# Block products of an attention-and-GLU kernel: from three phases of at most two weight sets to a phase of three and a phase of two

## The chip, the cores and the metric

The kernel runs on one NeuronCore of a Trainium2 chip. The metric is the device time of one execution in microseconds; the time before is the median of 3 runs. The engines are named as in the profile: PE (matrix products), DVE, ACT and POOL (elementwise work) and SP (which issues the DMAs).

## The reference

Attention over 4 batches x 8 heads x 768 rows x 64 columns, in which a query sees only the keys of its own hash bucket, and then a gated layer over 3072 tokens:

```python
q_bucket = sum((q @ proj > 0) * powers)            # 6 bits, the same for k
scores = where(q_bucket == k_bucket, q @ k.T / 8, -1e9)
x = softmax(scores) @ v                            # as (3072, 512)
gate = 1 / (1 + exp(-(x @ w_gate)))                # w_gate, w_val: 512 x 1536
return (gate * (x @ w_val)) @ w_out                # w_out: 1536 x 512
```

The weights arrive as 64-bit floats and are converted on the chip. Products are made with three matmuls each (a high part and a low part of both operands, low times low left out).

## The kernel before, in words

`Plan` is a list scheduler that runs while the program is built. Each piece of work is added with a key, an engine (or two, of which one is chosen), an estimated duration, what it comes after, and the tokens that it takes and gives (`stock` says how many there are). `Plan.order()` plays the estimates through and writes every engine's instructions in the order in which it started them. On the chip each engine then runs its own list in that order and waits on semaphores; the estimates have no other effect.

The first half is attention, in 32 units. Beside it the weights are converted: the 1536 columns of the hidden layer are 12 blocks `j` of 128. Blocks 0 and 1 stay in SBUF and are used beside attention (`moe_early`; tiles zg, zv, zo): they give each token's partial sum, written to the DRAM tensor `part`. Blocks 2 to 11 are five sets of two (`SETS`), stored in DRAM (`kept`) in a form for a block product: the tokens of a batch are two halves, the 512 inputs are two halves, and seven products of block sums (`STEPS`, tiles z1 to z7) stand for eight. `converted`, `combined` and `split` make that form. `QUARTERS` says how many sets are converted beside attention; the rest are converted later, beside the block products.

The block products are the second half. `PHASES` says which sets are worked on together; a phase goes over the four batches b, and one (phase, batch) is a pair, built by `moe_pair`:
- `x_pair` loads the four blocks of x (ra) and makes seven operand blocks a11, a12, s1, s2, s3, s4, a22, each in a high and a low part: 4 sums and 7 differences of 128x768, plus 7 casts on ACT;
- `group` runs the seven steps for g (the gate) and for v (the values) of one set: PE writes a z bank (six of them, tag z), ACT copies some out (sn), DVE adds others (L758), and `finish` makes the four results of 128x384: for g a sigmoid, for v the product with the gate (L772), its high part on ACT (gh, L787) and its low part (gl, L789). Where both "pool" and "dve" stand, the planner chooses;
- `part_` makes the output products (yo): 6 token tiles, and for each set 2 blocks x 3 matmuls of 128x512. `ended` fetches the tile's partial sum from DRAM (ob or ol, three buffers each), adds yo on DVE (L893) and stores it, in the last phase to the output.

A set's weights (10 pieces, 4.72 MB) lie in one of two slots and are fetched once per phase by `fetch_piece`. The places that the change and the prediction touch are these functions, the table `PHASES`, `QUARTERS`, and the token list.

Of the kernel before, what the change touches and what calls it, by code (L numbers as in the profile page):

```python
# [169 lines left out]
def lsh_attention_glu_kernel(ctx, tc, q, k, v, proj, w_gate, w_val, w_out, out):  # L170
# [13 lines left out]
    QUARTERS = 3  # L184
# [16 lines left out]
    PHASES = [SETS[i : i + 2] for i in range(0, len(SETS), 2)]  # L201
# [86 lines left out]
    def busy():  # L288
# [5 lines left out]
        ef=4, raw1=1, cv1=1, wk1=2, raw2=1, cv2=1, wk2=1, xr=1, x=1, ob=3, ol=3, sn=4, sg=6, gf=4, sc=1,  # L294
# [27 lines left out]
    def converted(key, n, j, late, which, after, first):  # L322
# [50 lines left out]
        b1 = add(key, "dve", 440, exponent, after=[a], take=[token] if first else [])  # L373
        b2 = add(key, "act", 700, shifted, after=[b1])
        c1 = add(key, "dve", 440, mantissa, after=[b1])
        c2 = add(key, "dve", 700, whole, after=[c1])
        d = add(key, "dve", 700, signed, after=[b2, c2], give=[raw_])
        return z, add(key, "pool", 1300, lambda: scaled(nc.gpsimd), after=[d])

    def split(key, src, to, size, late, after, give, tile_of=None):  # L380
# [17 lines left out]
        low_ = add(key, "pool", 100 + 1200 * part_, low, after=[h], give=give)  # L398
# [22 lines left out]
    def combined(key, n, js, late, after):  # L421
# [27 lines left out]
        x1 = add(key, on(t1), after=[ea, eb])  # L449
        x2 = add(key, on(t2), after=[x1])  # L450
        x3 = add(key, on(t3), after=[eb])
        x4 = add(key, on(t4), after=[x2, x3])
# [20 lines left out]
    def load_x(u, b, g, stored):  # L473
# [21 lines left out]
        for c in range(KC):  # L495
            prev = add(
                FIRST, "act", 415, lambda c=c: high(c), after=[a, prev], take=["x"] if c == 0 else []
            )
            z["ready"].append(add(
                FIRST,  # L500
                [("pool", 960, lambda c=c: low(c, nc.gpsimd)), ("dve", 470, lambda c=c: low(c, nc.vector))],
                after=[prev], give=["xr"] if c == KC - 1 else [],
            ))
# [25 lines left out]
    def gated(u, j, z, done, zsig):  # L529

        def mul():
# [9 lines left out]
            after=[b, g_free[j]],  # L541
# [74 lines left out]
    def x_pair(u, b, last_use):  # L616
# [35 lines left out]
        on = lambda fn: [("pool", 2000, lambda: fn(nc.gpsimd)), ("dve", 960, lambda: fn(nc.vector))]  # L652
# [7 lines left out]
        def summing(name, x, y, op, after):  # L660
            got[name] = add(
                FIRST, on(lambda eng: summed(name, x, y, op, eng)), after=[got[x], got[y]] + after,
                take=["sc"] * (name == "s1"),
            )

        def pieces_of(name):
            h = add(FIRST, "act", 850, lambda: high(name), after=[got[name]], take=[f"x{name}"])
            z["ready"][name] = add(FIRST, on(lambda eng: low(name, eng)), after=[h])
# [25 lines left out]
    pieces = {}  # L694

    def fetch_piece(js, slot, n, m, after, first):

        def go():
            size = HF if m == 3 else DM
            if slot == 1 and n != "o" and m < 3:  # L700
                to = w1.tile([P, 2, size], F32R, name=f"w{n}{m}_{js[0]}", tag=("wg0", "wg1", "wv0", "wv1", "wo0", "wo1")[3 * (n == "v") + m])
            else:
                to = later["x"].tile([P, 2, size], F32R, name=f"w{n}{m}_{js[0]}", tag=f"w{slot}{n}{m}")
# [4 lines left out]
        made[js, n, m] = dma(  # L708
            1e3, CROWDED if first else CROWDED // 4, go, after=[made_piece[key_], later["switch"]] + after, take=[f"w{slot}{n}{m}"]
# [7 lines left out]
    def group(key, u, n, js, slot, x, sig_, final, free_w, hslot, prev):  # L717
# [4 lines left out]

        z, bank, done, told = {}, {}, {}, {}
# [13 lines left out]
        def pe(m):  # L737
            block, piece, half = STEPS[m]
            give = [f"x{block}"] if final else []
            if free_w and m in (2, 6, 3, 4):  # L740
                give = give + [f"w{slot}{n}{piece}"]
            done[m] = add(
                key, "pe", 6 * MM, lambda: step(m), after=[prev, x["ready"][block], made[js, n, piece]], take=["z"], give=give,
# [20 lines left out]
        def finish(where):  # L764
            a = told[where]
            if n == "g":
# [6 lines left out]
            soon = slice(None, None, -1 if final and uu == 0 else 1)  # L773
            b = add(
                FIRST, [("pool", 1040, lambda: mul(nc.gpsimd)), ("dve", 480, lambda: mul(nc.vector))][soon],
                after=[a, sig_[where][1]], give=["sg"],
            )

            def hi():
# [12 lines left out]
                FIRST, [("pool", 1040, lambda: low_(nc.gpsimd)), ("dve", 480, lambda: low_(nc.vector))][soon],  # L792
                after=[c], give=["gf"],
            )

        for m in (1, 2, 5, 6, 3, 7, 4):
# [8 lines left out]
            elif m == 6:  # L805
# [4 lines left out]
                    FIRST, [("pool", 1040, lambda: both(nc.gpsimd)), ("dve", 480, lambda: both(nc.vector))],  # L810
                    after=[told["t"], told["u"]],
# [13 lines left out]
    def moe_pair(key, i, b, prev, before):  # L825
# [4 lines left out]

        sets, last_phase, last_pair = PHASES[i], i == len(PHASES) - 1, b == B - 1
        u = f"{i}_{b}"
        x = x_pair(u, b, None)
        alone = len(sets) == 1
        sigs = []
        for slot, js in enumerate(sets):
            sig_ = {}
            sigs.append(sig_)
            for n in "gv":
                final = slot == len(sets) - 1 and n == "v"  # L840
                prev = group(key, u, n, js, slot, x, sig_, final, last_pair, b % 2 if alone else slot, prev)
        accs = {}

        def part_(t, slot):
            hslot = b % 2 if alone else slot
            if slot == 0:
                accs[t] = ps.tile([P, 512], F32, name=f"yo{t}_{u}", tag="one")
            js = sets[slot]
            uu, tt = t // GT, t % GT
            ts_ = slice(tt * P, (tt + 1) * P)  # L850
            for jj in range(2):
                h_, l_ = hs[hslot, jj, uu]
                oh, ol = pieces[js, "o", jj]
                for q, (a, w) in enumerate(((l_, oh), (h_, ol), (h_, oh))):
                    nc.tensor.matmul(  # L855
                        accs[t], a[:, ts_], w, start=(slot == 0 and jj == 0 and q == 0),
                        stop=(slot == len(sets) - 1 and jj == 1 and q == 2),
                    )

        def out_part(t, slot, prev):  # L860
            uu = t // GT
            ready = [sigs[slot]["h", (jj, uu)] for jj in range(2)] + [made[sets[slot], "o", jj] for jj in range(2)]
            give = []
            if t % GT == GT - 1:
                give += [f"h{b % 2 if alone else slot}{jj}{uu}" for jj in range(2)]
            if last_pair and t == 2 * GT - 1:
                give += [f"w{slot}o{jj}" for jj in range(2)]
            return add(
                key, "pe", 6 * MO, lambda: part_(t, slot), after=[prev] + ready,
                take=["moe", "one"] if slot == 0 else [], give=give,  # L870
            )

        def ended(t, prev):
            z = {}
# [4 lines left out]
            def fetch():  # L879
                pool = mp if where == "ob" else later["t"]  # L880
                z["ob"] = pool.tile([P, DM], F32, name=f"{where}{t}_{u}", tag=where, bufs=stock[where])
                nc.sync.dma_start(z["ob"], part[b][g, tt])

            def store():
# [3 lines left out]
                nc.sync.dma_start(to, z["ob"])  # L888

            a = dma(FIRST, 262144, fetch, after=[parts[b, g, tt], later["switch"]] + in_turn[where], take=[where])  # L890
            in_turn[where] = [a]
            a = add(
                FIRST, "dve", 640, lambda: nc.vector.tensor_add(z["ob"], accs[t], z["ob"]), after=[prev, a],  # L893
                give=["moe", "one"],
            )
            parts[b, g, tt] = dma(FIRST, 262144, store, after=[a], give=[where])

        n_ = len(sets)
# [5 lines left out]
        def outs(prev):  # L904
            for o in order_:
                prev = out_part(*o, prev)
                if o[1] == n_ - 1:
                    ended(o[0], prev)
            return prev

        if not alone:
            return outs(prev), None
        if before:
            prev = before(prev)
        if last_pair:
            return outs(prev), None
# [366 lines left out]
```

## Time and profile before

| | |
|---|---|
| median of 3 runs | 1130.66 us (1125.63 to 1131.22) |
| profiled execution | 1125.4 us, span 1123.3 us |
| granted TensorE clock, mean | 0.971 |
| first block product starts | 574.3 us into the span |
| PE, DVE, ACT, POOL busy, share of the span | 92%, 78%, 51%, 41% |
| DMA moved | 181.23 MB |

The span is what the trace covers; the profiled execution's own time lies 2.1 us above it. A row of the trace for a matmul begins where it is issued and overlaps the next, so two starts give its cost. A wait row has the engine that waits, whom it waited for, the total, how often, and the longest.

### The profile page before, as it was taken

The numbers are of one execution on the slowest core, as the hardware profiler recorded it, in microseconds if no ns is written. First come the engines' busy times: TensorE is split into PE (matmuls) and PEld (weight loads), VectorE is DVE, ScalarE is ACT, GpSimd is POOL, SyncE is SP. The second block draws the span as 40 slices with busy tenths as digits, with TensorE's granted clock in tenths as the row PEclk, the third lists the DMA queues.
The fourth block names the chain that finished last, engine by engine and source line by source line (L and its number), as shares of the span: only waits on it lengthen the run. The fifth ranks groups of instructions, "written<-read, shape, count | busy, mean of one in ns | idle before, by whom it ended". The sixth has DMA issues, their size and how long they took to land.

```text
span 1123.3 us, 21291 instructions
## 1 busy us (share of the span) xinstructions
PE 1033.1 (92%) x8172; PEld 822.5 (73%) x8172; DVE 877.5 (78%) x1568; ACT 577.2 (51%) x1035; POOL 463.5 (41%) x358
## 2 busy tenths in 40 slices
PE   8999999999999999999897989798989898987888
PEld 5666666666676667666697878697979696977776
DVE  6888999999989877787358798969684756668774
ACT  2778777676886667566444253424332342414331
POOL 0012344344454101101356485738562535455652
PEclk9999999999999999999999999898989998998899
DMA  8245665747667334221686527287622314452435
GB/s 197 62 128 140 177 187 180 235 144 236 214 206 223 106 121 113 81 79 38 231 300 234 187 100 247 98 297 284 258 94 76 125 45 146 154 195 67 169 113 169
DMA packets 144773, 181.23 MB, mean 161 GB/s; under 512 B 63776, under 2 KB 104736, under 8 KB 144672
## 3 DMA queue, kind: packets, MB, share of 16 engines
q1 hardware_dynamic: 142944, 179.48, 49.7%
q8 instruction: 64, 1.05, 0.4%
q10 hardware_dynamic: 1728, 0.40, 0.2%
q14 instruction: 37, 0.30, 0.1%
HBM read 111.68 MB, written 55.57 MB: 149 GB/s over the span
## 4 chain that ended last, share of the span: by engine, by line
PE 53%; DVE 26%; issue 8%; DMA 5%; ACT 5%; POOL 3%; SPq 0%; DVEq 0%; POOLq 0%; ACTq 0%
PE yo L855 10%; PE pv L1136 8%; PE sc L1057 6%; PE tp L1119 4%; DVE e L1067 4%; PE sc L1051 3%; PE zv L517 2%; PE zo L550 2%; DVE ef L1126 2%; ACT e L1086 2%; PE zg L517 2%; DVE gf(1, 0)v L772 2%; PE z6g L733 1%; PE idle L289 1%; DMA rawg<-in_moe_w_gate_dram 1%
## 5 line engine op out<-in xcount | busy, mean ns | idle before, releaser
L1086 ACT ACTIVATE e<-e,st 128x768 f32<-128x768 f32 x192 | 196.3, 1024 | 70.6 <-DVE st L1079 70.2
L1067 DVE TENSOR_SCALAR_CACHE_REDUCE e<-sc 128x768 f32<-128x768 f32 x192 | 178.1, 951 | 19.2 <-PE sc L1057 18.1
L1136 PE MATMUL pv<-ef,vr 128*64 128x384 f32 x768 | 142.4, 497 | 0.1
L1146 POOL TENSOR_TENSOR xs<-xs,rb 128x384 f32<-128x384 f32 x32 | 33.7, 1052 | 219.7 <-ACT xs L1143 121.7
L1119 PEld LDWEIGHTS tp<-ident,e 64*128 64x128 f32 x2304 | 85.4, 139 | 42.1 <-issue 16.4
L1126 DVE COPY ef<-tp 128x768 f32<-128x768 f32 x100 | 94.2, 950 | 23.1 <-PE tp L1119 23.0
L1119 PE MATMUL tp<-ident,e 64*128 64x64 f32 x2304 | 99.2, 226 | 11.4 <-DVE ef L1126 4.0
L1057 PE MATMUL sc<-kh,qsl 64*128 64x384 f32 x192 | 90.7, 472 | 0.0
L1057 PE MATMUL sc<-kh,ql 64*128 64x384 f32 x192 | 90.7, 472 | 0.0
L1136 PEld LDWEIGHTS pv<-ef,vr 128*64 128x64 f32 x768 | 47.6, 136 | 53.5 <-issue 46.3
L1126 ACT COPY ef<-tp 128x768 f32<-128x768 f32 x92 | 71.5, 789 | 18.0 <-PE tp L1119 17.8
L1051 PE MATMUL sc<-kb,qb 64*128 64x384 bf16 x384 | 65.3, 333 | 9.3 <-DVE ef L1126 3.1
L1057 PE MATMUL sc<-kh,qsh 64*128 64x384 f32 x192 | 64.6, 337 | 0.0
L1057 PE MATMUL sc<-kh,qh 64*128 64x384 f32 x192 | 64.6, 336 | 0.0
L1057 PE MATMUL sc<-kl,qh 64*128 64x384 f32 x192 | 64.3, 335 | 0.0
L1057 PE MATMUL sc<-kl,qsh 64*128 64x384 f32 x192 | 64.3, 335 | 0.0
L1051 PEld LDWEIGHTS <-qb 64*128 64x128 bf16 x384 | 22.8, 95 | 50.4 <-issue 45.4
L893 DVE TENSOR_TENSOR ob<-yo,ob 128x512 f32<-128x512 f32 x36 | 24.7, 686 | 29.1 <-PE yo L855 26.8
L808 POOL TENSOR_TENSOR sntg<-sntg,snug 128x384 f32<-128x384 f32 x16 | 18.4, 1153 | 67.5 <-DVE snug L758 67.5
L753 ACT COPY snm1g<-z1g 128x384 f32<-128x384 f32 x20 | 9.6, 478 | 70.3 <-PE z1g L733 70.3
L893 DVE TENSOR_TENSOR ol<-yo,ol 128x512 f32<-128x512 f32 x36 | 24.6, 684 | 21.3 <-PE yo L855 18.1
L855 PE MATMUL yo<-wo,gh 128*128 128x512 f32 x120 | 40.0, 417 | 0.0
(624 smaller groups left out, 3274.6 us busy)
## 6 DMA issues: line engine op xcount, KB each, us to landing
ra<-xd SPq DMA_DIRECT2D x48, 384.0 KB
part<-ob SPq DMA_DIRECT2D x48, 256.0 KB
ol<-part SPq DMA_DIRECT2D x36, 256.0 KB
ob<-part SPq DMA_DIRECT2D x36, 256.0 KB
kg<-pkg SPq DMA_DIRECT2D x15, 512.0 KB
kv<-pkv SPq DMA_DIRECT2D x15, 512.0 KB
wg<-kg SPq DMA_DIRECT2D x15, 512.0 KB
wv<-kv SPq DMA_DIRECT2D x15, 512.0 KB
```

The lines of the kernel that those rows point to most:

```text
L517: nc.tensor.matmul(z["acc"][:, :GN], a[:, wc], x[xx][c // 2][:, c % 2, :], start=(c == 0 and i == 0), stop=(c == KC - 1 and i == 2),)
L550: nc.tensor.matmul(acc, a[:, slot, ts_], w, start=(first and i == 0), stop=(last and i == 2))
L855: nc.tensor.matmul(accs[t], a[:, ts_], w, start=(slot == 0 and jj == 0 and q == 0), stop=(slot == len(sets) - 1 and jj == 1 and q == 2),)
L893: FIRST, "dve", 640, lambda: nc.vector.tensor_add(z["ob"], accs[t], z["ob"]), after=[prev, a],
L1051: nc.tensor.matmul(sc[:, j, :GN], z["qb"][rows, c], z["kb"][rows, h], start=True, stop=False, tile_position=(j * D, 0),)
L1057: nc.tensor.matmul(sc[:, j, :GN], q_[rows, c], z["k" + x][rows, h * GN : (h + 1) * GN], start=False, stop=(m == 2), tile_position=(j * D, 0),)
L1067: nc.vector.tensor_scalar(sp(e), gz["sc", t, h][:, :, :GN], -SCALE, None, op0=ALU.mult, op1=ALU.min, accum_out=gz["st", t][:, 0, h : h + 1],)
L1086: nc.scalar.activation(e, e, AF.Exp, bias=st[:, 2, h : h + 1], scale=st[:, 1, h : h + 1], accum_out=gz["su"][:, h * GT + t : h * GT + t + 1],)
L1119: nc.tensor.transpose(tp[:, r, at_ : at_ + D], gz["e", t, h][rows, c * P : (c + 1) * P], ident[rows, rows], tile_position=(r * D, 0),)
L1126: copy(gz["ef", c].rearrange("p (n r d) -> p r n d", r=2, d=D), gz["tp", c][:, :, :GN].rearrange("p r (n d) -> p r n d", d=D),)
L1136: nc.tensor.matmul(gz["pv"][rows, :GN], z["v"][:, h, c], gz["ef", c][:, h * GN : (h + 1) * GN], start=(c == 0), stop=(c == NC - 1), tile_p ...
L1146: nc.gpsimd.tensor_mul(gz["xs"], gz["xs"], gz["rb"])
```

## The change

1. `PHASES` becomes one phase of three sets and one of two. In the phase of three, two sets share slot 1, so their weights are fetched anew in every pair; the third set keeps slot 0. In the first pair the set in slot 0 goes first.
2. In a pair of three, the output products of the first set of slot 1 are put behind gate and value products of a later set, and added to the partial sum there; the other two sets' follow at the end. In a pair of two both stand at the end. They are ordered by set and then by token tile, where before the two sets alternated per tile; six accumulators are open at once (two banks of tag one, four of tag z).
3. A partial sum tile is fetched and stored once per pair and phase: 48 times each instead of 72.
4. x sums, x differences, the product with the gate, the low part and the sum of t and u are no longer offered to POOL: they are DVE's. POOL keeps conversions and the early units' work.
5. A token `port` (one of it) is taken by every POOL operation and every DVE operation that reads and writes SBUF alone, so that the planner never starts two of them together. It adds no wait on the chip; it changes the order.
6. `QUARTERS` 4 instead of 3: four sets are converted beside attention, one later. Some estimates change (640 to 690 for the addition of yo, 1230 to 1050 for `divided`).

```diff
-    QUARTERS = 3
+    QUARTERS = 4
-    PHASES = [SETS[i : i + 2] for i in range(0, len(SETS), 2)]
+    PHASES = [[(SETS[0], 1), (SETS[1], 0), (SETS[2], 1)], [(SETS[3], 1), (SETS[4], 0)]]
...
-        on = lambda fn: [("pool", 2000, lambda: fn(nc.gpsimd)), ("dve", 960, lambda: fn(nc.vector))]
+        on = lambda fn: [("dve", 960, lambda: fn(nc.vector))]
...
-                FIRST, [("pool", 1040, lambda: mul(nc.gpsimd)), ("dve", 480, lambda: mul(nc.vector))][soon],
-                after=[a, sig_[where][1]], give=["sg"],
+                FIRST, [("dve", 480, lambda: mul(nc.vector))],
+                after=[a, sig_[where][1]], take=["port"], give=["sg", "port"],
...
+        leaves = lambda m: last_pair or any(sets[o][1] == sets[m][1] for o in range(n_) if o != m)
+        home = lambda m: 1 - sets[m][1]
...
+        def part_(t, m, start, stop):
+            if start:
+                pool, tag_ = (ps, "one") if t < 2 else (later["ps"], "z")
+                accs[t] = pool.tile([P, 512], F32, name=f"yo{t}_{m}_{u}", tag=tag_)
...
-        order_ = [(0, 0), (1, 0)]
-        for s_ in range(1, n_):
-            order_ += [(0, s_), (1, s_)]
-        order_ += [(t, s_) for t in range(2, 2 * GT) for s_ in range(n_)]
+        def outs(ms, first, last, prev):
+            for m in ms:
+                for t in range(2 * GT):
+                    prev = out_part(t, m, m == ms[0], m == ms[-1], prev)
+                    if m == ms[-1]:
+                        ended(t, prev, first, last)
             return prev
+        for m, (js, slot) in enumerate(sets):
+            sig_ = {}
+            sigs.append(sig_)
+            for n in "gv":
+                prev = group(key, at_, n, js, slot, x, sig_, m == n_ - 1 and n == "v", leaves(m), home(m), prev)
+                if n_ == 3 and (m, n) == ((1, "v") if sets[0][1] else (2, "g")):
+                    both = [o for o in range(3) if sets[o][1]]
+                    prev = outs(both[:1], True, False, prev)
+        return outs([0, 1] if n_ == 2 else [o for o in range(3) if o != both[0]], n_ == 2, True, prev)
...
+            for js, slot in sets:
+                alone = sum(x[1] == slot for x in sets) == 1
+                for n, m in PIECES:
+                    if alone and b:
+                        made[(i, b), js, n, m] = made[(i, 0), js, n, m]
+                    else:
+                        fetch_piece((i, b), js, slot, n, m, [last_early] if (i, b) == (0, 0) and slot == 1 else [], (i, b) == (0, 0))
```

On PE, at the end of a pair of two sets, this stands before (the second phase's last pair: sets 6 and 8; wo_6 and wo_8 are their output weights, gl and gh the results of set 6, gl(1, 0)8 a result of set 8):

```order
L733 MATMUL z4v_1_3_12758<-a22h_3_12314,wv_8_10931 128x384
L855 MATMUL yo_1_3_12770<-wo_6_11082,gl 128x512
L855 MATMUL yo_1_3_12770<-wo_6_11082,gh 128x512 x2
L855 MATMUL yo_1_3_12770<-wo_6_11086,gl 128x512
L855 MATMUL yo_1_3_12770<-wo_6_11086,gh 128x512 x2
L855 MATMUL yo_1_3_12784<-wo_6_11082,gl 128x512
L855 MATMUL yo_1_3_12784<-wo_6_11082,gh 128x512 x2
L855 MATMUL yo_1_3_12784<-wo_6_11086,gl 128x512
L855 MATMUL yo_1_3_12784<-wo_6_11086,gh 128x512 x2
L855 MATMUL yo_1_3_12770<-wo_8_11099,gl(0, 0)8_1_3_12743 128x512
L855 MATMUL yo_1_3_12770<-wo_8_11099,gh(0, 0)8_1_3_12742 128x512 x2
L855 MATMUL yo_1_3_12770<-wo_8_11111,gl(1, 0)8_1_3_12794 128x512
```

The first results of the second set are asked for after 12 products of the first. In the changed kernel PE has this at the end of a pair of two (sets 8 and 10; the last rows of the first set's 36 products and the first of the second's):

```order
L856 MATMUL yo_0_1_1_12839<-wo_8_10_12060,gl(1, 1)8_1_1_12648 128x512
L856 MATMUL yo_0_1_1_12839<-wo_8_10_12060,gh(1, 1)8_1_1_12647 128x512 x2
L856 MATMUL yo_0_1_1_12853<-wo_8_10_12044,gl(0, 1)8_1_1_12684 128x512
L856 MATMUL yo_0_1_1_12853<-wo_8_10_12044,gh(0, 1)8_1_1_12683 128x512 x2
L856 MATMUL yo_0_1_1_12853<-wo_8_10_12060,gl(1, 1)8_1_1_12648 128x512
L856 MATMUL yo_0_1_1_12853<-wo_8_10_12060,gh(1, 1)8_1_1_12647 128x512 x2
L856 MATMUL yo_0_1_1_12789<-wo_10_10_11966,gl(0, 0)10_1_1_12752 128x512
L856 MATMUL yo_0_1_1_12789<-wo_10_10_11966,gh(0, 0)10_1_1_12751 128x512 x2
L856 MATMUL yo_0_1_1_12789<-wo_10_10_11969,gl(1, 0)10_1_1_12810 128x512
```

All six token tiles of the first set now stand ahead of the second set's first result.

On DVE, at the same place before (from the last value group's third step to gl(1, 0); POOL has some of the pair's other operations in its own list):

```order
L758 TENSOR_TENSOR gf(1, 0)v_1_3_12767<-z3v_1_3_12733,sntv_1_3_12729 128x384
L650 TENSOR_TENSOR s3l_0_12779<-ra_0_12319,s3h_0_12765 128x768
L772 TENSOR_TENSOR gf(1, 0)v_1_3_12767<-gf(1, 0)v_1_3_12767,sg(1, 0)g_1_3_12680 128x384
L758 TENSOR_TENSOR gf(1, 1)v_1_3_12791<-z7v_1_3_12748,sntv_1_3_12729 128x384
L642 TENSOR_TENSOR ra_0_12380<-ra_0_12380,sc_0_12392 128x768
L789 TENSOR_TENSOR gl(1, 0)8_1_3_12794<-gf(1, 0)v_1_3_12767,gh(1, 0)8_1_3_12793 128x384
```

The row L650 s3l and the row L642 belong to the next pair's x. In the changed kernel DVE has this there:

```order
L762 TENSOR_TENSOR gf(1, 0)v_1_1_12783<-z3v_1_1_12754,sntv_1_1_12761 128x384
L651 TENSOR_TENSOR s1l_2_12787<-sc_2_12517,s1h_2_12765 128x768
L762 TENSOR_TENSOR gf(1, 1)v_1_1_12798<-z7v_1_1_12768,sntv_1_1_12761 128x384
L776 TENSOR_TENSOR gf(1, 0)v_1_1_12783<-gf(1, 0)v_1_1_12783,sg(1, 0)g_1_1_12695 128x384
L762 TENSOR_TENSOR snuv_1_1_12763<-z7v_1_1_12768,snuv_1_1_12763 128x384
L776 TENSOR_TENSOR gf(1, 1)v_1_1_12798<-gf(1, 1)v_1_1_12798,sg(1, 1)g_1_1_12705 128x384
L762 TENSOR_TENSOR gf(0, 1)v_1_1_12813<-z4v_1_1_12776,snuv_1_1_12763 128x384
L792 TENSOR_TENSOR gl(1, 0)10_1_1_12810<-gf(1, 0)v_1_1_12783,gh(1, 0)10_1_1_12809 128x384
```

Most of the next pair's x work moved behind gl(1, 0), and POOL's products with the gate (L772, now L776) moved into DVE's list.

On SP, in the second pair of the phase of three, the fetches of the second set of slot 1 stand among partial sums and the late conversion's loads:

```order
L706 DMA wg_6_01_9940<-kg_0_120 128x1024
L706 DMA wg_6_01_9951<-kg_1_121 128x1024
L882 DMA ob_0_1_9955<-part_99 128x512
L706 DMA wg_6_01_9964<-kg_3_123 128x512
L338 DMA rawv_9967<-in_moe_w_val_dram 128x4x256
L882 DMA ol_0_1_9978<-part_99 128x512
L402 DMA kv_0_148<-pkv_0_148_9921 128x1024
L706 DMA wg_6_01_9990<-kg_2_122 128x1024
```

Before, no weights of the sets in use were fetched in a phase's second pair: SP had x loads, partial sums and the later sets' conversions there.

More of the change, by code (lines that the diff above doesn't have):

```diff
@@ L397, in split @@
         h = add(key, "act", 60 + 500 * part_, high, after=after, take=[wk] if tile_of is None else [])
-        low_ = add(key, "pool", 100 + 1200 * part_, low, after=[h], give=give)
+        low_ = add(key, "pool", 100 + 1200 * part_, low, after=[h], take=["port"], give=give + ["port"])
         if tile_of is not None:
@@ L540, in gated @@
             FIRST, [("pool", 960, lambda: low(nc.gpsimd)), ("dve", 470, lambda: low(nc.vector))],
-            after=[b, g_free[j]],
+            after=[b, g_free[j]], take=["port"], give=["port"],
         )
@@ L667, in pieces_of @@
             h = add(FIRST, "act", 850, lambda: high(name), after=[got[name]], take=[f"x{name}"])
-            z["ready"][name] = add(FIRST, on(lambda eng: low(name, eng)), after=[h])
+            z["ready"][name] = add(FIRST, on(lambda eng: low(name, eng)), after=[h], take=["port"], give=["port"])
         def release(what, *after):
@@ L707, in fetch_piece @@
         key_ = ("o", js[m]) if n == "o" else (n, js[0], m)
-        made[js, n, m] = dma(
-            1e3, CROWDED if first else CROWDED // 4, go, after=[made_piece[key_], later["switch"]] + after, take=[f"w{slot}{n}{m}"]
+        role = f"w{slot}{n}{m}"
+        made[at_, js, n, m] = last_fetch[role] = dma(
+            1e3, CROWDED if first else CROWDED // 4, go,
+            after=[made_piece[key_], later["switch"], last_fetch.get(role)] + after, take=[role],
         )
@@ L742, in pe @@
             done[m] = add(
-                key, "pe", 6 * MM, lambda: step(m), after=[prev, x["ready"][block], made[js, n, piece]], take=["z"], give=give,
+                key, "pe", 6 * MM, lambda: step(m), after=[prev, x["ready"][block], made[at_, js, n, piece]], take=["z"], give=give,
             )
@@ L915, in moe_pair @@
-        if last_pair:
-            return outs(prev), None
-        return prev, outs
+                nc.sync.dma_start(to, obs[t])
+            if first:
+                a = dma(FIRST, 262144, fetch, after=[parts[b, g, tt], later["switch"]] + in_turn[where], take=[where])
+                in_turn[where] = [a]
+                ended_[t] = a
+            ended_[t] = add(
+                FIRST, "dve", 690, lambda: nc.vector.tensor_add(obs[t], accs[t], obs[t]), after=[prev, ended_[t]],
+                give=["moe", "one"] if t < 2 else ["z"],
+            )
```

120 lines of the change are left out of this document (47 added, 73 removed).

## Prediction

> **What bounds the kernel now.** I read the page's first rows, then the table of stretches, then PE's waits, then the chain.
>
> ```profile
> span 1123.3 us, 21291 instructions
> PE 1033.1 (92%) x8172; PEld 822.5 (73%) x8172; DVE 877.5 (78%) x1568; ACT 577.2 (51%) x1035; POOL 463.5 (41%) x358
> DMA packets 144773, 181.23 MB, mean 161 GB/s; under 512 B 63776, under 2 KB 104736, under 8 KB 144672
> ```
>
> PE is busy 92% over all, but attention and the block products have different limits. The block products run from the first z1g to the last yo:
>
> ```profile
> 574.31 0.33 PE L733 MATMUL z1g<-a11h,wg 128*128 128x384 f32 x1
> 1117.86 0.62 PE L855 MATMUL yo<-wo,gh(1, 1)10_2_3_13773 128*128 128x512 f32 x2
> ```
>
> That is 544.2 us (574.31 to 1118.48). One pair of the second phase, split into its first set, its second set and its 72 output products (columns: stretch, length, busy us of PE, PEld, DVE, ACT, POOL, granted clock, DMA share, GB/s):
>
> ```profile
> 952.78:967.34 14.56, 14.56 (x86) 14.56 (x85) 7.25 (x13) 4.28 (x9) 3.66 (x4) 1.00 0.75 256
> 967.34:981.90 14.56, 14.56 (x86) 14.56 (x85) 9.73 (x16) 8.53 (x16) 8.20 (x7) 1.00 0.20 65
> 981.90:1005.04 23.14, 18.26 (x74) 14.61 (x73) 16.97 (x18) 3.94 (x6) 13.08 (x7) 0.93 0.49 163
> ```
>
> The gate and value products run without a gap. The output products take 23.14 us, and the rows of PE there show the work in it:
>
> ```profile
> 981.77 0.39 PE L855 MATMUL yo<-wo,gl 128*128 128x512 f32 x1
> 984.53 0.39 PE L855 MATMUL yo<-wo,gl(0, 0)8_1_3_12743 128*128 128x512 f32 x1
> 990.25 0.80 PE L855 MATMUL yo<-wo,gl(1, 0)8_1_3_12794 128*128 128x512 f32 x1 [4.88 <-DVE gl(1, 0)8_1_3_12794 L789]
> ```
>
> Twelve products from 981.77 to 984.53 are 0.23 us each, so 72 cost 16.6 us; the pair loses 6.6 us: 4.9 us waiting for gl(1, 0) of the second set, the rest at a lower clock right after. So PE's content of the stage is 20 set-passes x 14.56 = 291.2, plus 720 x 0.23 = 165.6, plus 18 output products of the early units that stand in between (4.1): 461 us. The stage loses 83 us. PE's waits from 532 us on (18 rows, the four largest here) are nearly all at yo:
>
> ```profile
> PE yo L855 <- DVE ol L893: 12.3, 6, 3.9
> PE yo L855 <- DVE gl(1, 0)4_0_2_10424 L789: 6.7, 1, 6.7
> PE yo L855 <- DVE gl(1, 0)4_0_0_9413 L789: 6.2, 1, 6.2
> PE yo L855 <- DVE gl(1, 0)8_1_0_11437 L789: 4.9, 1, 4.9
> ```
>
> What makes gl(1, 0) late is DVE behind POOL. Durations, minimum/median/maximum, of DVE's pair operations:
>
> ```profile
> L772 DVE TENSOR_TENSOR gf(1, 0)v<-gf(1, 0)v,sg(1, 0)g x13: 545/2149/2159, 612.7 to 1075.9; 128x384 f32<-128x384 f32 x13
> L650 DVE TENSOR_TENSOR s3l<-ra,s3h x10: 943/2346/2352, 667.2 to 1073.7; 128x768 fp32r<-128x768 f32 x10
> L758 DVE TENSOR_TENSOR sg(1, 0)g<-z3g,sntg x20: 545/558/560, 584.2 to 1092.7; 128x384 f32<-128x384 f32 x20
> ```
>
> The same multiplication is 545 ns or 2149 ns. An operation that reads PSUM (third row) never stretches. The long ones lie where POOL works:
>
> ```profile
> 984.65 2.52 POOL L650 TENSOR_TENSOR a22l<-ra,a22h 128x768 fp32r<-128x768 f32 x1
> 985.44 2.15 DVE L772 TENSOR_TENSOR gf(1, 0)v<-gf(1, 0)v,sg(1, 0)g 128x384 f32<-128x384 f32 x1
> ```
>
> DVE's 2.15 us end 0.42 us after POOL's end at 987.17: it waited for POOL and then ran.
>
> **The change part by part.**
>
> *Output order.* The first set's 36 products (8.3 us) now stand ahead of the second set's at each pair's end; before, only 12 (2.8 us) stood there. DVE's queue from gf(0, 0) of the last value group to gl(0, 1) is 18 operations: 15 of 0.55 and 3 of 0.95 us, 11 us, starting when z2v ends, 2.1 us into a 7.3 us group. It ends 5.9 us after the group, ahead of the 8.3. gl(1, 0), four places earlier, has 5 us to spare. In the phase of three the extra 36 products stand a set behind their own products. So I cost the waits at nothing; their cover is those 8.3 us, and without it they return at 6.6 us per pair. Late next would be the x blocks of the next pair: 6 operations x 0.95 and 6 additions x 0.69 follow, 9.8 us, and 5.9 + 9.8 = 15.7 against yo's 16.6 us; the last block is needed only 6 us into the next group, so that fits.
>
> *PSUM.* Six accumulators instead of two; four come from the six z banks. The third is needed 2.8 us after the group, when its bank (z2v's) was emptied long since. The ol wait (12.3 us in the row above, two banks) goes. Cost 0.
>
> *Pair work on DVE.* Instructions in the block stage: 101 of DVE and 99 of POOL become 200 of DVE; the x work goes from 132 (66 each) to 88, since four x pairs go. DVE per set-pass: 22 x 0.55 = 12.1 us; per x pair 11 x 0.95 = 10.4; 6 additions of 0.69 for each of one or two output passes:
>
> ```profile
> L893 DVE TENSOR_TENSOR ob<-yo,ob 128x512 f32<-128x512 f32 x36 | 24.7, 686 | 29.1 <-PE yo L855 26.8
> ```
>
> Phase of two: 24.2 + 10.4 + 4.1 = 38.7 us of PE's 45.7 (29.1 + 16.6). Phase of three: 36.3 + 10.4 + 8.3 = 55 of 68.5 (43.7 + 24.8). DVE fits, if nothing stretches it.
>
> *The set still converted late* (two before, one now) leaves 24 operations on POOL in phase one, at up to 1.3 us:
>
> ```profile
> L369 POOL TENSOR_TENSOR exo<-mfo,exo x4: 1286/1290/1301, 684.4 to 801.1; 128x512 f32<-128x512 f32 x4
> ```
>
> That is up to 31 us in which DVE's pair operations stand. DVE itself has four conversion operations for each of the set's six operands, two like either of these rows, 6 x 2.2 = 13 us:
>
> ```profile
> L364 DVE SCALAR_TENSOR_TENSOR exo<-rawo,exo x4: 680/681/683, 683.6 to 799.6; 128x512 int32<-128x512 int32 x4
> L354 DVE TENSOR_SCALAR mfo<-rawo x4: 416/418/2072, 680.5 to 798.1; 128x512 int32<-128x512 int32 x4
> ```
>
>  The slack over the three pairs it spreads through is 3 x 13.5 = 40 us. Bounds 0 and 31 us; I take 8, near the low end, since slack covers nearly all of it. [...]
>
> *Weights fetched again.* Fetches go from 50 to 110, x loads from 48 to 32, partial sums from 72 in and 72 out to 48 each. A pair of three then moves two sets of 4.72 MB, 1.6 of x and 3.1 of sums: 9.4 + 4.7 = 14.2 MB in 68.5 us, 207 GB/s. DMA has done more:
>
> ```profile
> 592.00:596.00 4.00, 4.00 (x25) 4.00 (x24) 3.81 (x8) 0.86 (x2) 1.90 (x2) 1.00 1.02 403
> ```
>
> A set takes 12 us at that rate. It is needed 29 us or more after its slot begins to free in the usual pair, and 12.5 us after in the first pair, where g alone (1.8 MB, 5 us) is due then. On SP's queue each fetch waits for PE's last use and holds the x loads and sum fetches behind it; those have a whole set-pass. Cost 0 to 10; I take 0.
>
> *First pair.* Its x work is all on DVE, with POOL's early splits beside it. Bounds 0 and 10 us (11 operations of 0.95); I take 3, since PE still has early products to run. For the remaining seven pairs I add 4 in all for handovers.
>
> *Attention.* A fourth set is converted there. POOL's L369 shows 24 conversions between 56 and 392 us, six to a set, so a set takes 84 us:
>
> ```profile
> 336.00:364.00 28.00, 2.56 (x2) 1.00 0.72 226
> 364.00:392.00 28.00, 1.27 (x1) 1.00 0.35 107
> sum 560.00, POOL 30.71; mean POOL 1.54
> ```
>
> PE's waits from 100 to 370 us are 11 rows, 14.1 us in all, and from 380 to 530 us only two:
>
> ```profile
> PE tp L1119 <- DVE e L1067: 2.6, 5, 0.9
> PE sc L1051 <- DVE kb L1004: 0.3, 1, 0.3
> ...
> PE sc L1051 <- DVE ef L1126: 0.6, 2, 0.4
> PE tp L1119 <- DVE ef L1126: 0.3, 1, 0.3
> ```
>
> 84 x (14.1/270 - 0.9/150) = 4 us more; bounds 0 and 13 (DVE's conversions of a set wholly on the path). The port token only reorders, and could take or give some of that: 0.
>
> *End.* After the last product come one addition and one store, as now (4.8 us).
>
> Sum of the span: 574.3 + 4 + 461 + (8 + 3 + 4) + 4.8 = 1059. Around the span lie 2.1 us (the profiled execution took 1125.4): 1061. The median of the runs before, 1130.66, is 5.3 above that execution and the lowest run 0.2 above, so I add 2: **1063 us**.
>
> **The rivals.**
> - *DVE becomes the bound.* For it: 80 to 85% of PE's time is already owed, with waits on ACT between. Against: DVE runs 27.66 of 28 us in one stretch:
>
> ```profile
> 700.00:728.00 28.00, 21.27 (x109) 19.55 (x108) 27.66 (x35) 12.97 (x24) 20.38 (x14) 0.93 0.29 98
> ```
>
> If it costs each of eight pairs 3 us, or the late set's 31 us of POOL fall on it whole: 1087.
> - *Slower: the weights come late.* If fetches move only at the page's mean, 161 GB/s, a pair of three takes 14.2/0.161 = 88 us, 19.5 more than PE; four pairs, +78: 1141. It is slower than before when a pair takes over 87 us, below 163 GB/s. Against: 403 GB/s above; the mean is what was asked for.
> - *The change doesn't do what it says*: gl(1, 0) stays the last to come. 8 x 6.6 = 53: 1116. For it: DVE has twice the pair work. Against: the count of 11 us.
> - *Attention pays for the fourth set*, 13 instead of 4 us: 1072.
> - *PE's clock.* After a wait the granted clock falls:
>
> ```profile
> 936.00:940.00 4.00, 2.98 (x7) 2.40 (x8) 4.00 (x5) 1.07 (x2) 2.57 (x2) 0.50 0.26 93
> 896.00:924.00 28.00, 28.00 (x158) 27.41 (x157) 13.90 (x24) 9.57 (x20) 8.30 (x8) 1.00 0.20 63
> ```
>
> If changing through more banks made many short pauses, the stage could run at 0.93 as in the output stretch above: 461/0.93 is +35: 1098. Against: 28 us without a pause at 1.00 while z's banks go round. [...]
>
> **How the numbers follow.** Forecast 0.70 (own range 1048 to 1078, from the bounds above); DVE the bound 0.11; attention 0.07; the waits stay 0.05; weights late 0.05 (0.03 of it slower); clock 0.02. From 1046 to 1087 lie the forecast, attention and most of DVE's case: 0.85. A measurement of this kernel can tell about 0.5% from no change. Faster 0.95, same 0.02, slower 0.03.
>
> **What would show it.** Right: PE's waits for gl at yo gone, the clock 1.00 through whole pairs, pairs of 68 to 70 and 46 us; L776 on DVE near 545 ns in phase two and stretched only in phase one; DVE above 80% after 575 us; POOL empty in the second half. Wrong: PE waiting at z1g for a DMA (weights), at z5g or z6g for s1l or s2l (DVE), or the first z1g later than 582 us (attention).

## The result and the profile after

| | before | changed |
|---|---|---|
| median of 4 runs, us | 1129.23 | 1042.23 (1041.62 to 1049.79) |
| profiled execution, us | 1125.4 | 1042.39 |
| span of the trace, us | 1123.3 | 1040.1 |
| start of the second set's products, us | 593.09 | 592.57 |

The changed kernel takes 0.9248 of the time before (95% interval 0.9199 to 0.9298). It was forecast faster, at 1063 us; it came 21 us lower, 4 us under the lower end of the range of 1046 to 1087 us and 6 us under that of the forecast's own case, 1048 to 1078.

The head of the page:

```profile
span 1040.1 us, 21145 instructions
PE 1003.7 (97%) x8169; PEld 807.7 (78%) x8172; DVE 817.0 (79%) x1658; ACT 557.2 (54%) x1008; POOL 227.2 (22%) x223
DMA packets 142148, 190.66 MB, mean 183 GB/s; under 512 B 63712, under 2 KB 100576, under 8 KB 142048
```

PE is busy for 97% of a shorter span, and POOL's work has halved. The table of stretches, from the first block product to the last, with two pairs of two between the last rows left out (columns as before: length, busy us of PE, PEld, DVE, ACT, POOL, clock, DMA share, GB/s):

```profile
566.19:592.57 26.38, 26.38 (x145) 25.35 (x145) 17.76 (x29) 13.02 (x25) 5.23 (x4) 1.00 0.84 287
592.57:647.67 55.10, 54.28 (x277) 49.36 (x277) 44.66 (x80) 21.24 (x39) 8.05 (x8) 1.00 0.77 281
647.67:717.26 69.59, 68.90 (x361) 63.90 (x360) 54.91 (x97) 26.48 (x50) 14.32 (x12) 1.00 0.71 259
717.26:785.56 68.30, 68.30 (x362) 64.00 (x360) 53.44 (x95) 23.85 (x45) 2.77 (x2) 1.00 0.62 217
785.56:853.85 68.29, 68.29 (x361) 64.00 (x360) 50.94 (x89) 22.55 (x43) 0.00 (x0) 1.00 0.79 276
853.85:899.36 45.51, 45.51 (x242) 42.66 (x240) 35.70 (x61) 16.70 (x31) 0.00 (x0) 1.00 0.37 133
...
990.37:1036.04 45.67, 45.67 (x241) 42.47 (x239) 26.71 (x50) 11.28 (x24) 0.00 (x0) 1.00 0.20 67
```

A pair of two takes 45.5 us where it took 52 to 53 in the second phase before, at a clock of 1.00. The first row holds 11.8 us of the early units' products beside the first set (before, 4.2). So the start of the stage alone misleads (566.19 against 574.31); the start of the *second* set has all early products behind it in either kernel, and there the two differ by 0.5 us. PE's waits from 560 us to the end, all of them:

```profile
PE z4g L737 <- DVE snuv L762: 0.8, 1, 0.8
PE zo L551 <- POOL gl L539: 0.7, 1, 0.7
PE z3g L737 <- DVE snuv L762: 0.4, 1, 0.4
PE z6g L737 <- DVE gf(1, 0)v L762: 0.3, 1, 0.3
```

There is no wait at yo and none for a DMA. In a pair of two, rows of DVE and of PE show how early the result that PE used to wait for now is:

```profile
930.85 0.55 DVE L792 TENSOR_TENSOR gl(1, 0)10_1_1_12810<-gf(1, 0)v,gh(1, 0)10_1_1_12809 128x384 fp32r<-128x384 f32 x1
937.38 0.39 PE L856 MATMUL yo<-wo,gl(1, 0)10_1_1_12810 128*128 128x512 f32 x1
```

It is done at 931.4, 6.0 us before it is used (the prediction said 5). The last value group ended at 928.5, so it is 2.9 us late against that, where it was 8.5 us before.

### The profile page after: what moved, and what is told of

Read it like the earlier page. It is cut to its first block, busy times and chain, and to the rows that moved or that the text cites. A ratio compares the mean times of both kernels' runs of the same rounds, so it can differ in the third digit from the quotient of the medians.

```text
span 1040.1 us, 21145 instructions
## 1 busy us (share of the span) xinstructions
PE 1003.7 (97%) x8169; PEld 807.7 (78%) x8172; DVE 817.0 (79%) x1658; ACT 557.2 (54%) x1008; POOL 227.2 (22%) x223
## 4 chain that ended last, share of the span: by engine, by line
PE 75%; DVE 10%; ACT 6%; DMA 5%; issue 2%; SPq 1%; POOL 0%; DVEq 0%; ACTq 0%; POOLq 0%
PE yo L856 15%; PE pv L1136 9%; PE sc L1057 6%; PE tp L1119 5%; DVE e L1067 4%; ACT e L1086 3%; PE zg L518 3%; PE zv L518 3%; PE sc L1051 2%; PE zo L551 2%; DMA rawv<-in_moe_w_val_dram 2%; PE z4g L737 2%; PE z1g L737 2%; PE z1v L737 2%; PE z4v L737 2%; PE z7v L737 2%
## 5 line engine op out<-in xcount | busy, mean ns | idle before, releaser
L1126 DVE COPY ef<-tp 128x768 f32<-128x768 f32 x90 | 84.6, 950 | 21.0 <-PE tp L1119 20.9
L1126 ACT COPY ef<-tp 128x768 f32<-128x768 f32 x102 | 79.0, 792 | 17.6 <-PE tp L1119 17.1
L856 PE MATMUL yo<-wo,gh 128*128 128x512 f32 x144 | 44.6, 391 | 0.0
L518 PE MATMUL zg<-xh,wg 128*128 128x384 f32 x128 | 38.8, 358 | 2.2 <-ACT xh L488 2.2
L1057 PEld LDWEIGHTS sc<-kh,ql 64*128 64x128 f32 x192 | 37.2, 194 | 0.0
```

Source lines behind the costliest of these rows:

```text
L518: nc.tensor.matmul(z["acc"][:, :GN], a[:, wc], x[xx][c // 2][:, c % 2, :], start=(c == 0 and i == 0), stop=(c == KC - 1 and i == 2),)
L856: nc.tensor.matmul(accs[t], a[:, ts_], w, start=(start and jj == 0 and q == 0), stop=(stop and jj == 1 and q == 2),)
L1057: nc.tensor.matmul(sc[:, j, :GN], q_[rows, c], z["k" + x][rows, h * GN : (h + 1) * GN], start=False, stop=(m == 2), tile_position=(j * D, 0),)
L1126: copy(gz["ef", c].rearrange("p (n r d) -> p r n d", r=2, d=D), gz["tp", c][:, :, :GN].rearrange("p r (n d) -> p r n d", d=D),)
```

## The experiments

Theory A: the waits at yo came from two things together, DVE stretched by POOL and an output order that asks for the second set after 2.8 us, and taking away either is enough. Rivals: only the order counts (B), only DVE counts (C), the phases bring the gain (D).

**The parts undone in the changed kernel.** Old order of the output products, DVE still alone:

```diff
-            for m in ms:
-                for t in range(2 * GT):
+            seq = [(t, m) for m in ms for t in (0, 1)] + [(t, m) for t in range(2, 2 * GT) for m in ms]
+            for t, m in seq:
...
```

> The changed kernel, with the output products of the last two sets of a pair alternating per token tile again (the second set's first product is asked for after 12 products, 2.8 us, of the first). In the changed kernel's trace gl(1, 0) of the second set is ready 2.9 us after the last value group, and the old order would ask for it 3.4 us after it. Theory A (either part alone is enough: DVE freed of POOL is early enough for the old order): no wait of more than 0.5 us per pair comes back, 1042 to 1048 us, pairs of two at 45.5 to 46.5 us. Rival B (the order is what removed the waits): some 5 to 6.6 us per pair come back in seven pairs, 1077 to 1088 us.

Pair work offered to POOL again (so too for the other four lines of that kind), no token:

```diff
-sc=1, port=1,
+sc=1, port=99,
...
-        on = lambda fn: [("dve", 960, lambda: fn(nc.vector))]
+        on = lambda fn: [("pool", 2000, lambda: fn(nc.gpsimd)), ("dve", 960, lambda: fn(nc.vector))]
```

> The changed kernel, with the pair work offered to POOL again and the port token made ineffective (99 instead of 1); the new output order stays. Before the change gl(1, 0) came 8.5 us after the last value group; the new order asks for it 9.0 us after it. Theory A: the order alone covers the stretched DVE, the waits at yo stay below 2 us per pair, 1042 to 1056 us. Rival C (DVE without POOL is what removed the waits): DVE runs late, 5 to 7 us per pair come back, 1077 to 1091 us.

Both of these edits:

> The changed kernel with both undone: old alternating order of the output products, pair work offered to POOL, no port token; the phases of three and two stay. Theory A (either alone is enough, both are not needed, but with neither the waits return): 6.6 us per pair in seven pairs, 1080 to 1095 us, PE waiting at yo for gl(1, 0) again. Rival D (the gain came from the phases, that is from fewer single-set pairs, x pairs and partial sums): 1042 to 1055 us.

**The same parts alone in the kernel before.** DVE alone (the pool entries struck out):

> The kernel before, with the pair work on DVE alone (x sums and differences, the product with the gate, the low part, the sum of t and u no longer offered to POOL); phases, output order and everything else as before. Theory A: the eight pairs of two, which lose 60 us beside the content, lose at most 10; the phase of one set owes DVE 26.6 us a pair (12.1 + 10.4 + 4.1) against PE's 22.8 and loses 15 of its 22 still: 1068 to 1080 us. Rival B (the output order is needed): the waits at yo stay, 1110 to 1130 us.

The order alone (six accumulators, set by set):

```diff
-        order_ = [(0, 0), (1, 0)]
-        for s_ in range(1, n_):
-            order_ += [(0, s_), (1, s_)]
-        order_ += [(t, s_) for t in range(2, 2 * GT) for s_ in range(n_)]
+        order_ = [(t, s_) for s_ in range(n_) for t in range(2 * GT)]
```

> The kernel before, with the output products set by set and six accumulators open; pair work still offered to POOL, phases as before. Theory A: gl(1, 0), 8.5 us after the last value group in the trace of before, is asked for at 9.0 us: most of the 60 us of the pairs of two goes, the phase of one set keeps its 22: 1070 to 1090 us. Rival C (DVE without POOL is what matters; a late DVE then delays the next pair's x blocks instead): 1105 to 1130 us.

Both:

> The kernel before with both: pair work on DVE alone and output products set by set with six accumulators; phases (2, 2, 1), three sets converted beside attention, no port token. Theory A: the same as the better of the two alone, within 8 us, 1062 to 1078 us; what is left to the changed kernel (some 20 to 30 us) is the phase of one set, in which DVE owes 26.6 us a pair to PE's 22.8. Rival D (the phases bring little): 1042 to 1052 us. Rival: the parts add up rather than overlap, below both by over 20 us.

Measured, median us, and in brackets one pair of two, from the table of stretches (the other pairs of two without conversions lie within 0.2 us of it, but for the last of all; with the old order and POOL they spread from 52.2 to 53.6):

| | pair work on DVE and POOL | on DVE alone |
|---|---|---|
| phases of before, old order | 1129.23 (52.26) | 1076.71 (46.64) |
| phases of before, new order | 1102.16 (47.54) | 1062.21 (45.51) |
| new phases, old order | 1103.69 (52.25) | 1040.88 (45.50) |
| new phases, new order | 1072.82 (47.57) | 1042.23 (45.51) |

The left column and the whole of the first two rows are without the token, which is the next experiment, and the first row has two accumulators where the others have six. The token also moves the end of attention, so the order and the engine are better compared in the part behind it, from the start of the second set to the end of the last product:

| us from the second set to the last product | pair work on DVE and POOL | on DVE alone |
|---|---|---|
| phases of before, old order | 525.4 | 476.6 |
| phases of before, new order | 499.8 | 458.4 |
| new phases, old order | 499.5 | 442.3 |
| new phases, new order | 468.9 | 443.5 |

With the new phases and DVE alone the order is worth nothing that can be measured: against the kernel before, the ratio of the whole times is 0.9233 (0.9207 to 0.9258) with the old order and 0.9248 (0.9199 to 0.9298) with the new. So B falls, and A is right for DVE.

For the order A is wrong: in the new phases, where POOL has pair work, the new order takes away 31 of the 56 us that the stage loses and leaves 25, 2 us in a pair of two and 2 to 7 in a pair of three. Its two runs, 1072.82 and 1102.16 us, lie above A's bands, and that with both undone, 1103.69, lies above its band too. C is wrong as well, since the order alone is worth those 31 us (26 in the phases of before). In the phases of before, with two accumulators and no token, DVE alone also left something for the order, 18 us behind the second set's start and 14.5 of the whole time: PE still waits there 7.7 us for gl(1, 0) and 7.7 us for an output tile. What the new order leaves beside POOL is in part a wait that I had not counted. PE's waits with POOL back (four of twelve rows):

```profile
PE yo L857 <- DVE gl(0, 1)6_0_0_9838 L793: 3.4, 1, 3.4
PE yo L857 <- POOL gl(0, 1)6_0_2_11262 L793: 2.0, 1, 2.0
...
PE yo L857 <- POOL gl(0, 1)10_1_0_12418 L793: 1.8, 1, 1.8
PE yo L857 <- POOL gl(0, 1)10_1_1_12865 L793: 1.7, 1, 1.7
```

It is not gl(1, 0), which I compared with its cover, but gl(0, 1), the last piece. With both undone the old wait is back (two of ten rows):

```profile
PE yo L857 <- DVE gl L793: 21.7, 4, 7.1
PE yo L857 <- DVE gl(1, 0)10_1_1_12816 L793: 4.9, 1, 4.9
```

The pair operations show why. The groups of one multiplication, POOL back and changed kernel (count, then busy us and mean ns; the first within 600 to 1070 us, the second within 566 to 1041), and a difference of 128x768 in the same two (minimum/median/maximum ns):

```profile
L776 DVE TENSOR_TENSOR gf(1, 0)v<-gf(1, 0)v,sg(1, 0)g 128x384 f32<-128x384 f32 x7 | 13.7, 1958 | 0.0
```
```profile
L651 DVE TENSOR_TENSOR s3l<-ra,s3h x7: 942/2346/2352, 642.6 to 1005.4; 128x768 fp32r<-128x768 f32 x7
```
```profile
L776 DVE TENSOR_TENSOR gf(1, 0)v<-gf(1, 0)v,sg(1, 0)g 128x384 f32<-128x384 f32 x20 | 11.1, 557 | 0.3
```
```profile
L651 DVE TENSOR_TENSOR s3l<-ra,s3h x8: 947/949/1143, 577.1 to 984.4; 128x768 fp32r<-128x768 f32 x8
```

D holds for a part. Between "before with both" (1062.21) and the changed kernel lie 20 us, but these two differ in the token and in the fourth conversion as well. The run with three sets and no token (1048.93, below) has the same order, engines and conversions as "before with both", but the new phases (and some new estimates): so the phases are worth 13 us, 4 of them ahead of the second set (597.14 against 593.07). The trace of "before with both" shows where as much is lost, in its phase of one set:

```profile
951.24:1055.53 104.29, 95.12 (x481) 86.52 (x479) 86.59 (x144) 39.54 (x69) 0.00 (x0) 0.98 0.47 156
```

Its content is 58.2 + 33 = 91, so it loses 13 us: 9.2 us of waits, and the rest in products that took longer (PE was busy 95.1 us), at a mean clock of 0.98 over the stretch. All four rows of its waits are for x blocks of the pair; the two largest in sum:

```profile
PE z2g L733 <- DVE a12l L650: 4.9, 3, 2.3
PE z3g L733 <- DVE s4l L650: 2.4, 3, 0.9
```

With one set, a pair has too few products to cover the next pair's x work. The 26.6 us of DVE that I set against PE's 22.8 are too many, however: DVE was busy 86.6 us, 21.6 a pair; the waits come because x is wanted at the pair's start.

**Token and conversions.** The token made ineffective (99 instead of 1), then three sets beside attention, then both, then five:

> The changed kernel, with the port token made ineffective (99 instead of 1); the pair work stays on DVE. If the token only reorders beside attention and the late conversion: within 3 us of the changed kernel, 1040 to 1046 us, the first block product within 3 us of 566. If it is what kept the fourth conversion from costing anything beside attention: attention longer by the 4 us that the prediction charged, or up to 13, 1046 to 1055 us.

> The changed kernel with three sets converted beside attention instead of four, so two late sets and 48 POOL operations of conversion (some 60 us of POOL) in the phase of three. If these cost what the prediction charged (8 us for 24 operations): +8 us or more in the stage, against up to 4 us less in attention, 1046 to 1054 us. If DVE's slack covers them altogether, as one late set showed: 1038 to 1045 us, stage within 2 us of its content. If the second late set's weights come too late for the phase of two: PE waits at z1g for wg, over 1055 us.

> The changed kernel with three sets converted beside attention and the port token made ineffective; only the start of the block products is read from it (with the token and three sets 563.1 us, with four 566.2; without the token and with four 573.4). If the token is worth the same 7 us with three sets: first block product at 569 to 571.5 us. If the token pays only for the fourth set's conversion: 563 to 566 us. PE's wait for wo<-ko of the second late set, 15.0 us with three sets, should be there again: 1055 to 1068 us.

> The changed kernel with all five sets converted beside attention, so POOL has no conversion left in the block stage. The step from three to four moved the first block product from 563.1 to 566.2 us; a fifth should move it to 569 to 572. In the stage the late set cost at most the 1.3 us by which the first pair of three after it (69.6 us) exceeds the next (68.3): 1043 to 1048 us. If the late set had cost the 8 us that the prediction charged, the stage would be 8 us shorter: 1035 to 1040 us.

The medians were 1050.24 (1047.95 to 1051.6), 1057.48, 1048.93 and 1077.1 us. What attention cost is read at the start of the second set, where all early products are done. The first set's stretch, no token with four sets, token with three, neither:

```profile
573.43:599.81 26.38, 26.38 (x145) 25.36 (x145) 16.16 (x27) 12.42 (x24) 4.96 (x4) 1.00 0.82 288
```
```profile
563.14:589.54 26.40, 26.40 (x145) 25.38 (x145) 17.76 (x29) 13.02 (x25) 5.24 (x4) 1.00 0.82 280
```
```profile
566.67:593.07 26.40, 26.40 (x146) 25.38 (x145) 16.32 (x27) 12.42 (x24) 4.97 (x4) 1.00 0.82 294
```

So the fourth set costs 599.81 - 593.07 = 6.7 us without the token and 592.57 - 589.54 = 3.0 with it; the token gives 7.2 us with four sets and 3.5 with three. Three sets without the token start where the kernel before did (593.07, 593.09). In the run with three and no token the start came at 566.67, between my two bands; the prediction of a wait for wo did not come true there, and its stage was longer by other waits.

In the other two totals a transfer decides. Late weights had been named as a possibility for three sets with the token (at z1g; they came late at yo), and not at all for five, whose total missed both of its bands. The first row is of three sets with the token, the second of five:

```profile
PE yo L856 <- DMA wo<-ko: 15.0, 1, 15.0
```
```profile
PE z1g L737 <- DMA wg<-kg: 32.2, 1, 32.2
```

With three, PE wants the last piece of the second late set at 891 us, and its store to DRAM is issued only at 900. With five, the fetches of the phase's weights are issued from 584 us on, behind the fifth conversion's loads and stores; in the changed kernel they start at 549. The stage of the run with five, once running, gives the late set's price. From the second set to the end of the first pair, then the second pair:

```profile
626.28:679.99 53.71, 53.71 (x278) 49.42 (x278) 40.90 (x72) 18.05 (x34) 0.00 (x0) 1.00 0.62 194
679.99:748.28 68.29, 68.29 (x362) 64.00 (x360) 50.91 (x89) 22.68 (x43) 0.00 (x0) 1.00 0.59 203
```

Against 55.10 and 69.59 in the changed kernel: 1.4 + 1.3 = 2.7 us for 24 POOL operations. The 1.4 may hold some of the first pair's own cost, since with five sets DVE had PE's wait of 32.2 us to get ahead. With two late sets the pair with as much POOL in it took 69.56. In the other runs of the changed kernel with one late set these two pairs lose between nothing (the early work on DVE, below) and 3.8 us (no token), so the price depends on the order.

**How much DVE has to spare.** Each x difference made twice, and thrice, the order unchanged:

```diff
-            eng.tensor_sub(z["l", name], z["r", name], f(z["h", name]))
+            for _ in range(2):
+                eng.tensor_sub(z["l", name], z["r", name], f(z["h", name]))
```

> The changed kernel, with each of the seven x differences of a pair (128x768 on DVE, L651) made twice: 7 more DVE operations of 0.87 to 0.95 us per pair, order unchanged. DVE then has 35.7 + 6.4 = 42 us of 45.5 in a pair of two and 54 + 6.4 = 60 of 68.3 in a pair of three; gl(1, 0) comes 0.9 us later of 6.0 spare. Theory (what DVE does behind its slack costs nothing; the prediction's 15 us for the late set, the first pair and handovers were charges for covered work): 1040 to 1046 us. Rival (at 85 to 92% DVE is already the bound through its waits on ACT, the prediction's first rival): 3 us for each of seven pairs, 1060 to 1066 us.

> The same with each difference made three times, 14 more operations, 12.2 to 13.3 us per pair. DVE owes 35.7 + 12.4 = 48.1 us or more in a pair of two, above PE's 45.5, and 54 + 12.4 = 66.4 of 68.3 in a pair of three. Theory: the pairs of two take 48 to 49.5 us where a next pair's x follows (three of them), those of three 68.3 to 70: 1048 to 1060 us, with PE waiting at the z groups for DVE. Rival (DVE has more room than the busy time says): below 1046 us.

1052.4 us (1050.16 to 1053.59) and 1109.69 (1107.55 to 1111.67): both above the theory's bands, the first below its rival's. One pair of two, twice and thrice:

```profile
909.01:955.46 46.45, 46.07 (x241) 42.58 (x240) 41.74 (x69) 16.81 (x31) 0.00 (x0) 1.00 0.32 101
```
```profile
938.92:992.84 53.92, 48.27 (x242) 44.78 (x240) 48.53 (x76) 16.74 (x32) 0.00 (x0) 0.94 0.28 88
```

The first 6.0 us of DVE cost 0.9 us a pair, the next 6.8 cost 7.5, more than their own length: PE stands still for 5.7 us of the pair (0.4 with the differences twice), and its mean clock is 0.94. Half of the 10 us of the first run came in one pair, that with the late conversion (74.94 us against 69.59). So the first rival of the prediction, DVE as the bound at 3 us a pair, comes true between 6 and 13 us more of DVE a pair. The new wait in the second run is not for x alone: a z bank still holds an output tile that DVE has not added.

```profile
PE z6g L738 <- DVE ol L896: 21.0, 6, 3.5
PE z3g L738 <- DVE ob L896: 7.0, 5, 2.1
```

**Why the token helps.** Without the token, and the early low parts and block sums offered to POOL alone; then with the token, and the same offered to DVE alone:

```diff
-                [("pool", 960, lambda c=c: low(c, nc.gpsimd)), ("dve", 470, lambda c=c: low(c, nc.vector))],
+                [("pool", 960, lambda c=c: low(c, nc.gpsimd))],
```

> The changed kernel without the port token, and with the early units' low parts (xl, gl) and the four block sums of each weight conversion offered to POOL alone. Without the token DVE does 10 of the xl, 3 of the gl and 9 of the block sums in the first 556 us, 18.0 us in all, and DVE is busy 19 us longer than with it; with the token POOL does all of them. Theory P (the token's 7 us come from where it puts this work, off DVE): first block product at 565 to 568.5 us, in all 1040 to 1046 us. Rival N (they come from not starting POOL's and DVE's operations together): first block product at 571 to 575 us, 1047 to 1052 us.

> The changed kernel with the port token, and the same work offered to DVE alone: some 30 xl, 14 gl and 32 block sums of 0.4 to 0.55 us move from POOL to DVE, 35 us. Theory P: attention grows by more than without the token, first block product at 574 to 585 us, 1050 to 1062 us. Rival N: with nothing overlapping, DVE's operations are short and the start moves by less than 3 us, 563 to 569 us, 1039 to 1046 us.

1042.6 us (1041.48 to 1045.93) and 1046.69 (1042.04 to 1048.75). The starts of the first block product, 574.77 and 583.25, don't fit the bands, because in these two kernels nearly all early products stand ahead of it; my bands took the start with 11.8 us of them behind. At the second set, where that falls out:

```profile
574.77:593.62 18.85, 18.85 (x103) 17.93 (x103) 10.18 (x19) 8.85 (x17) 4.13 (x4) 1.00 0.88 313
```
```profile
583.25:602.02 18.77, 18.77 (x103) 17.98 (x103) 13.14 (x24) 8.52 (x16) 0.00 (x0) 1.00 0.88 307
```

Without the token but with its placement the second set starts at 593.62: 6.2 of the 7.2 us are back, although POOL and DVE may start together there and DVE is busy 8.8 us longer in the first 556 us than in the changed kernel (465.2). With the token but without its placement it starts at 602.02: none of the 7.2 us, and 2.2 more are lost. So the token's gain is that it put this work on POOL, off DVE, which attention needs (P), and not that the two engines no longer start together (N). In time alone the second run is not clear of the changed kernel, since their ranges overlap, and its median lies under P's band of 1050 to 1062; what decides is the start of the second set. DVE was busy for 456.4 us of the first 556 in the changed kernel and 475.0 without the token; the moved operations account for 17.5 of these (10 xl 7.9, 3 gl 2.9, 8 block sums 6.7; the 18.0 of the expectation counted one too many). The token is not quite on every DVE operation that works in SBUF alone: the short ones of the softmax (`scale_`, `bias_`, `inverse`) do not take it.

## Why the prediction was right or wrong

| term, us | predicted | measured |
|---|---|---|
| attention and first set against before | +4 | -0.5 |
| PE's content of the stage | 461 | 459.3 |
| late set 8, first pair 3, handovers 4 | 15 | 2.9 |
| after the last product | 4.8 | 4.1 |
| from span to median | 4.1 | 2.1 |

The differences are 4.5 + 1.7 + 12.1 + 0.7 + 2.0 = 21 us.

- **Waits at yo at nothing: right.** None is left. But the reason given, the 8.3 us of cover, isn't needed: once DVE is freed of POOL, in the new phases the old order asks for gl(1, 0) 0.5 us after it is ready, and costs nothing.
- **The 15 us in the stage: the step that failed most.** They were three charges for work that I had just shown to lie behind slack (38.7 us of DVE against 45.7). Measured: 2.7 us for the late set and the first pair together, 0 for the handovers; 0.2 us more in the last pair (45.67 against 45.51) make the 2.9. POOL's work was about as large as counted (30.4 us for 26 operations from 566 us on), so it was the price that failed and not the amount. DVE had even less to do than counted, 35.7 and 51 us instead of 38.7 and 55; it was busy for 76% of the time after 575 us, where the prediction looked for over 80%, and no L776 took more than 622 ns, where it looked for stretched ones in the first phase.
- **The port token at 0: wrong.** I took it for a change of order; it changed which engine got the work, -7.2 us. The fourth set at +4 was a fair size: 3.0 with the token, 6.7 without. The term of -0.5 is the token's -3.5 with three sets and the fourth set's +3.0.
- **From the span to the median:** adding 2 us because the profiled execution lay low among the runs before was no better than adding nothing; here it lay 0.2 us from the median.
- **The price of a product:** 0.23 us, rounded, over 720 products. A pair of two holds 45.51 - 29.12 = 16.39 us of them, 0.2276 each, and with that and 4.2 us of early products the content is 291.2 + 163.9 + 4.2 = 459.3.
- **POOL's work charged to DVE:** the upper bound put all 31 us of the late set's POOL work on DVE. In the stretch with 14.32 us of POOL, DVE was busy 54.91 us, 4 us more than in the pair without (50.94), conversions included. Single operations did stretch beside POOL's pair work (s3l, median: 2346 ns with POOL back, 949 in the changed kernel), and those that read PSUM did not (in the trace of before all 240 of L758 took 542 to 560 ns, all 72 of L893 671 to 693); charged over a whole stage the 31 us are a bound, far from what happened.
- **Rivals.** DVE the bound, 1087: not so, but between 6 and 13 us of DVE a pair away. Weights late, 1141: the changed kernel moved 217 to 281 GB/s in the pairs of three without a wait for a DMA; late weights did decide the runs with three and five sets, by when they were asked for and not by the rate (with five, up to 398 GB/s from 584 us on while PE waited). Attention pays 13: without the token it would have paid 6.7. The clock stayed at 1.00 in every pair.

No run was faster than the changed kernel by more than its range. The old order (with the token), and the early work on POOL without a token (with the new order), do as well (1040.88 and 1042.6): each of the two can be left out of the changed kernel. Both left out together were not tried.

## What to carry to other kernels

When a profile shows an operation at two durations (545 and 2149 ns), look first for an engine that was at work beside the long ones: here taking POOL out of the pair work (1129.23 to 1076.71 us in the phases of before) was worth more than the new order of the products (1102.16), and in the new phases that one edit did what two were made for. Work that a count shows to lie behind slack is charged nothing in the sum, and its full price goes into the range instead. A token or rule for a planner is read in the order that it makes: count, for each engine, which operations moved there.

## What had not been expected of the hardware

- The slack has a hard edge: 6.0 us more of DVE in a pair cost 0.9 us, 6.8 more cost 7.5, of which PE stood still for 5.3, and the clock was 0.94 over the pair where it had been 1.00.
- A two-input DVE operation (L776, gf(1, 0)v) slowed to 1958 ns on average beside POOL's pair work, though POOL's own busy time in a pair of two was only 22.8 of 47.6 us; 14.3 us of POOL in a pair of three, in the changed kernel, left the same operation at 557 ns over the whole stage. What sets them apart, a queue of POOL work side by side with DVE's against single operations that wait for DVE themselves (in the changed kernel POOL stood 96.5 us from 566 us on, in six waits, for DVE's exg, exv and exo), was not tried by itself. It is hardly the token: in the run without it, in the first two pairs of three with 22.1 us of POOL, 21 of 22 products with the gate took 539 to 557 ns and one 1095.
